# Moving the time operands to the other half of the TensorE array, and reordering the start of a chunked RWKV-7 + MoE kernel

## The chip, the cores and the metric

The kernel runs on one core of a Trainium2 chip, as one launch. The metric is the device time in microseconds; the median of three runs before the change is 947.24 us (946.98 to 950.19).

## The reference

Two blocks run one after the other. The first is an RWKV-7 recurrence over 4 batches, 8 heads, 768 steps and a head size of 40: each head keeps a 40x40 state, which in every step is decayed by `w`, corrected by `a` and `b`, and extended by `v` and `k`; the output of a step reads the state with `r`.

```python
for t in range(S):
    y[:, :, t] = einsum('bhd,bhde->bhe', rt, state)
    Sa = einsum('bhde,bhe->bhd', state, at)
    state = state * wt - outer(Sa, bt) + outer(vt, kt)
```

Its output, 3072 rows of 320, goes through a mixture of 8 experts (320 to 1024, ReLU, and back to 320). The expert of a row is the argmax of its logits, and the result is scaled by the softmax weight of that expert.

## The kernel before, in words

**The recurrence** is computed in 12 chunks of 64 steps. In a chunk the work is split into two units (`s` = 0, 1), each with two batches and eight heads, laid out as 8 groups `g` times two partition halves `par`. A unit's matrices are 64x64 or 64x40 per head. Partition half 0 holds one head and half 1 another, so every small product uses one 64x64 quarter of the 128x128 TensorE array: its rows are given by the partitions of the operands, its columns by the partitions of the output. The helpers `own(par)` and `oth(par)` name a half and the other half. A product that reads `own` and writes `own`, or reads `oth` and writes `oth`, uses one of the two quarters on the array's diagonal; one that reads `own` and writes `oth`, or the reverse, uses one of the two off the diagonal. A step of a unit is a group of 16 products (8 groups, 2 halves); each fp32 product shows in the trace as two MATMULs and two LDWEIGHTS.

**Two streams** are interleaved on TensorE by `weave` (L532), which writes out TensorE's program order by hand. One is the system of the next chunk, `systems` (L571): per unit `ntb`, five steps `level(u, k)`, `couple` and `whole`, 16 groups in all, which invert a triangular 64x64 matrix; the units alternate. `level`, `couple` and `whole` read and write the same half (diagonal quarters); `ntb` is off the diagonal. The other stream is `rest` (L583), 26 groups: `right`, `gtk`, `solve`, `zgram`, `state`, `yield_y`, `atv`, `turned`, `emit`. Two products of `rest` are followed by 16/26 as many of the system.

Before the change `gtk` (L271), `atv` (L289), the first group of `state` (the product of `nk` and `nv`, L450) and the first groups of `yield_y` (with `s_r`, L487, and with `nk` and `AT`, L490) lie on the diagonal, the same quarters as the levels. `right`, `solve`, `zgram` and the second groups of `state` and `yield_y` (with `nb`) lie off it. Where groups from two row halves accumulate into one PSUM bank, `parted` (L212) puts a small ScalarE copy between them, which the second group waits for.

**The chain of a level**: ScalarE copies the new power out of PSUM (L356), VectorE transposes it (`new_n`, L309), VectorE adds the product to the running inverse (L359); the next level of the same unit reads both.

**Decay** (L243) runs ahead for later chunks: a scan on VectorE gives the cumulative decay `PT` (L247), four reciprocals give `wi` (L258), GpSimd multiplies `a` into `ai` (L253) and `k`, `b` into `kb` (L260). `ntb` and `gtk` need `ai` and `kb`.

**The start.** All constants and presets are written on GpSimd: masks, the counters that only the router needs (L87 to L110), zero or one padding of partitions 40 to 63 in the load tiles (L153 to L159), identity columns (L170), zero columns (L173). All input loads are issued on SyncE's queue: per unit 4 for `wp`, 4 for `a`, 8 for `kb` (`load`, L219), 8 for `v` and `ri` (`load_vr`, L231), 40 KB each. Then the system of chunk 0 is woven with `gtk` and `atv` of chunk 0 (L602).

Only TensorE's order is written by hand (`manual_schedule`, L596); on the other engines and queues a planner orders the instructions by when it reckons them ready, earlier code first.

Of the kernel before, what the change touches and what calls it, by code (L numbers as in the profile page):

```python
# [8 lines left out]
F32 = mybir.dt.float32  # L9
# [4 lines left out]
ALU = mybir.AluOpType  # L14
# [3 lines left out]
W, K, A, B_, V, R = range(6)  # L18
# [3 lines left out]
def kernel(  # L22
# [51 lines left out]
    after = consts.tile([128, 128], F32)  # L74
    nc.gpsimd.memset(after[:], 1.0)
    nc.gpsimd.affine_select(
        after[:], after[:], compare_op=ALU.is_gt, fill=0.0, base=0, pattern=[[-1, 128]], channel_multiplier=1,
    )
    ones_sq = consts.tile([128, 128], F32)
    nc.gpsimd.memset(ones_sq[:], 1.0)  # L80
    zero_e = consts.tile([128, E], F32)
    nc.gpsimd.memset(zero_e[:], 0.0)
    keep = consts.tile([128, E, NT], F32)
    nc.gpsimd.memset(keep[:], 1.0)
    nc.gpsimd.memset(keep[:, :, 0:1], 0.0)

    def counted(name, shape, pattern, base, mult=0):  # L87
        ti = consts.tile(shape, I32, name=name + "_i")
        tf = consts.tile(shape, F32, name=name)
        nc.gpsimd.iota(ti[:], pattern=pattern, base=base, channel_multiplier=mult)  # L90
        nc.gpsimd.tensor_copy(tf[:], ti[:])
        return tf

    first_w = counted("first_w", [128, E], [[-1, E]], E)
    b1off = counted("b1off", [128, E], [[CAP, E]], -1)
    b2off = counted("b2off", [128, E], [[-CAP, E]], E * CAP - CAP)
    thr = counted("thr", [128, NX], [[128, NX]], CAP)
    kx = counted("kx", [1, NX], [[1, NX]], 0)
    iota_f = counted("iota_f", [128, 128], [[1, 128]], 0)

    tokv = counted("tokv", [128, NT], [[2 * S, B // 2], [64, S // 64]], 1, 1)
    nc.gpsimd.tensor_scalar(tokv[64:], tokv[64:], scalar1=float(S - 64), scalar2=None, op0=ALU.add)
    iota_r = consts.tile([128, 128], F16)
    nc.gpsimd.tensor_copy(iota_r[:], iota_f[:])

    tok_n = consts.tile([128, NT // 2], F32)
    nc.gpsimd.tensor_scalar(
        tok_n[:], tokv[:, NT // 2 :], scalar1=-1.0, scalar2=float(N // 2), op0=ALU.mult, op1=ALU.add,
    )
    nc.gpsimd.tensor_copy(tokv[:, NT // 2 :], tok_n[:])  # L110
# [8 lines left out]
    with tc.tile_pool(name="ring", bufs=1) as ring, \  # L119
         tc.tile_pool(name="sb", bufs=1) as sb, \  # L120
         tc.tile_pool(name="pp", bufs=1, space=PSUM) as pp:

# [38 lines left out]
        nc.gpsimd.memset(first[:], 0.0)  # L161
        nc.gpsimd.memset(first[:, :, 0:1], 1.0)
# [6 lines left out]
        for t in sum(ai_r + ri_r, []):  # L169
            nc.gpsimd.tensor_copy(t[:, :, T2:], i40[:, None, :].to_broadcast([128, G, D]))  # L170

        for t in sum(nk_r + st_r + s_r + q_r, []):
            nc.gpsimd.memset(t[:, :, D:], 0.0)  # L173
        for t in sum(off_r, []):
            nc.gpsimd.memset(t[:], 0.0)
        for t in sum(x_r, []):
            nc.gpsimd.tensor_copy(t[:], i64[:, None, :].to_broadcast([128, G, T2]))
# [10 lines left out]
        for par in range(2):  # L188
            nc.gpsimd.tensor_copy(iw[own(par), :, :D], i40[own(par), None, :].to_broadcast([64, NP, D]))
# [686 lines left out]
```

## Time and profile before

| | us |
|---|---|
| runs, median of 3 | 947.24 (946.98 to 950.19) |
| profiled execution, its own time | 950.85 |
| span of its instructions | 949.0 |
| PE busy | 847.2 (89%) |
| PEld busy | 659.7 (70%) |
| DVE busy | 404.0 (43%) |
| POOL busy | 281.4 (30%) |
| ACT busy | 261.1 (28%) |

PE is TensorE's matmuls, PEld its weight loads, DVE VectorE, ACT ScalarE, POOL GpSimd, SP SyncE; a q behind a name is the engine's queue issuing. The span runs from the first instruction to the last; the 1.85 us between it and the run's own time lie around it. Matmuls overlap, so a busy PE only says that some matmul was in flight, not how many quarters of the array worked. The page cuts the span into 40 slices of 23.7 us and gives the busy share of each in tenths.

### The profile page before, as it was taken

The numbers are of one execution on the slowest core, as the hardware profiler recorded it, in microseconds if no ns is written. First come the engines' busy times: TensorE is split into PE (matmuls) and PEld (weight loads), VectorE is DVE, ScalarE is ACT, GpSimd is POOL, SyncE is SP. The second block draws the span as 40 slices with busy tenths as digits, with TensorE's granted clock in tenths as the row PEclk, the third lists the DMA queues.
The fourth block names the chain that finished last, engine by engine and source line by source line (L and its number), as shares of the span: only waits on it lengthen the run. The fifth ranks groups of instructions, "written<-read, shape, count | busy, mean of one in ns | idle before, by whom it ended". The sixth has DMA issues, their size and how long they took to land.

```text
span 949.0 us, 37272 instructions
## 1 busy us (share of the span) xinstructions
PE 847.2 (89%) x16828; PEld 659.7 (70%) x16828; DVE 404.0 (43%) x711; ACT 261.1 (28%) x686; POOL 281.4 (30%) x299
## 2 busy tenths in 40 slices
PE   0298798999999999999999991999999999999995
PEld 0288788999999999999999991353635455453633
DVE  1274858584857667585853616210111201011100
ACT  0045252535344353534345330010111001010110
POOL 9634432624325161623422013302113030210101
PEclk9998999999999999999999995799999999999998
DMA  2304132322222232322101008222224131322000
GB/s 63 74 7 91 31 79 51 86 58 59 49 64 63 49 75 46 73 45 59 39 20 38 4 18 245 74 70 92 75 86 146 67 105 63 95 73 62 21 0 22
DMA packets 119605, 60.16 MB, mean 63 GB/s; under 512 B 103825, under 2 KB 115091, under 8 KB 119444
## 3 DMA queue, kind: packets, MB, share of 16 engines
q1 hardware_dynamic: 113236, 48.53, 19.8%
q0 software_dynamic: 3072, 9.20, 3.1%
q8 instruction: 133, 2.18, 1.0%
q10 hardware_dynamic: 3136, 0.01, 0.2%
q14 instruction: 28, 0.23, 0.1%
HBM read 49.83 MB, written 9.19 MB: 62 GB/s over the span
## 4 chain that ended last, share of the span: by engine, by line
PE 38%; issue 35%; POOL 10%; DVE 8%; DMA 3%; ACT 3%; SPq 1%; POOLq 0%; DVEq 0%; ACTq 0%
PE ps_lv L208 12%; PE ps_y L208 6%; POOL out_dram L799 3%; PE ps_ntb L208 3%; PE ps_q L208 3%; POOL xg L761 2%; PE ps_s L208 2%; PE ps_x L208 2%; PE ps_atv L208 2%; PE ps_f L208 2%; PE ps_gtk L208 2%; DVE N L309 2%; DVE pair L359 2%; PE ps_S L208 2%; DVE wi L258 2%
## 5 line engine op out<-in xcount | busy, mean ns | idle before, releaser
L208 PE MATMUL ps_lv<-pair,N 64*64 64x128 f32 (+1 forms) x3840 | 292.8, 256 | 13.2 <-DVE pair L359 8.4
L208 PEld LDWEIGHTS ps_lv<-pair,N 64*64 64x64 f32 x3840 | 249.6, 135 | 18.3 <-issue 12.6
L780 PE MATMUL hp<-xgT,w 128*128 128x512 f32 (+1 forms) x384 | 191.9, 629 | 0.0
L780 PEld LDWEIGHTS hp<-xgT,w 128*128 128x128 f32 (+1 forms) x384 | 63.3, 189 | 123.3 <-issue 122.1
L793 PE MATMUL zp<-w,h_sb 128*128 128x320 f32 x512 | 145.0, 433 | 0.0
L309 DVE STREAM_TRANSPOSE N<-pair 128x512 f32<-128x512 f32 x144 | 101.5, 705 | 96.8 <-ACT pair L356 95.5
L785 DVE TENSOR_SCALAR h_sb<-hp 128x512 f32<-128x512 f32 x32 | 22.1, 692 | 247.1 <-PE hp L780 247.1
L793 PEld LDWEIGHTS zp<-w,h_sb 128*128 128x128 f32 x512 | 94.5, 191 | 34.5 <-issue 0.8
L799 POOL DMA_INDIRECT out_dram<-zo,s_idx x32 | 31.8, 995 | 279.9 <-ACT zo L798 279.9
L208 PE MATMUL ps_ntb<-ai,kb 40*64 40x104 f32 x768 | 73.4, 279 | 45.7 <-POOL kb L260 45.7
L208 PEld LDWEIGHTS ps_ntb<-ai,kb 40*64 40x64 f32 x768 | 61.4, 146 | 46.1 <-POOL kb L260 46.1
L299 POOL TENSOR_TENSOR AT<-AT,up 128x512 f32<-128x512 f32 x24 | 30.5, 1271 | 203.1 <-ACT AT L298 181.1
L258 DVE RECIPROCAL wi<-PT 128x128 f32<-128x128 f32 x96 | 81.6, 907 | 0.6
L356 ACT COPY pair<-ps_lv 128x512 f32<-128x512 f32 x96 | 57.6, 600 | 63.3 <-PE ps_lv L208 52.6
L787 ACT ACTIVATE h_sb<-hp 128x512 f32<-128x512 f32 x32 | 19.1, 597 | 200.5 <-PE hp L780 200.5
L260 POOL TENSOR_TENSOR kb<-kb,wi 128x512 f32<-128x512 f32 x48 | 65.9, 1390 | 26.8 <-DVE wi L258 24.5
L208 PE MATMUL ps_y<-N,off 64*64 64x64 f32 x768 | 63.4, 223 | 5.8 <-DVE N L309 5.7
L208 PE MATMUL ps_gtk<-ai,kb 40*64 40x104 f32 x768 | 68.2, 260 | 0.2 <-issue 0.2
L359 DVE TENSOR_TENSOR pair<-ps_lv,pair 128x512 f32<-128x512 f32 x96 | 63.2, 659 | 8.2 <-PE ps_lv L208 7.3
L208 PEld LDWEIGHTS ps_y<-N,off 64*64 64x64 f32 x768 | 56.2, 133 | 8.2 <-PE ps_y L208 6.2
L208 PE MATMUL ps_atv<-ri,v 40*64 40x104 f32 x768 | 58.5, 251 | 0.2 <-issue 0.2
L208 PEld LDWEIGHTS ps_gtk<-ai,kb 40*64 40x64 f32 x768 | 57.2, 139 | 0.3 <-issue 0.3
(161 smaller groups left out, 1484.8 us busy)
## 6 DMA issues: line engine op xcount, KB each, us to landing
w<-in_moe_w_dram SPq DMA_DIRECT2D x8, 1280.0 KB
w<-in_moe_w_dram SPq DMA_DIRECT2D x8, 1024.0 KB
kb<-in_packed_dram SPq DMA_DIRECT2D x192, 40.0 KB
v<-in_packed_dram SPq DMA_DIRECT2D x96, 40.0 KB
ri<-in_packed_dram SPq DMA_DIRECT2D x96, 40.0 KB
a<-in_packed_dram SPq DMA_DIRECT2D x96, 40.0 KB
wp<-in_packed_dram SPq DMA_DIRECT2D x96, 40.0 KB
x_rows<-xr SPq DMA_DIRECT2D x48, 80.0 KB
```

Of the source, the lines that this page charges most:

```text
L208: nc.tensor.matmul(out_, lhsT=lhs, rhs=rhs, start=start, stop=stop, skip_group_check=free)
L258: nc.vector.reciprocal(wi[:, h, p : p + 2], P4[:, h, p : p + 2, 1:])
L260: nc.gpsimd.tensor_tensor(d["kb"][:, :, i], d["kb"][:, :, i], wi[:], op=ALU.mult)
L299: nc.gpsimd.tensor_tensor(t[:], t[:], up64[:, None, :].to_broadcast([128, G, T2]), op=ALU.mult)
L309: nc.vector.transpose(flat(N[:]), flat(nt))
L356: nc.scalar.copy(new[:, 0], ps[:, :, :T2])
L359: nc.vector.tensor_tensor(new[:, 1], ps[:, :, T2:], pair[:, 1], op=ALU.add)
L780: nc.tensor.matmul(hp[:, :cols], lhsT=g["w"][0][:dsz, db, fb * 128 : (fb + 1) * 128], rhs=g["xT"][:dsz, db, :cols], start=(db == 0), stop= ...
L785: nc.vector.tensor_relu(g["h"][:, fb, :cols], hp[:, :cols])
L787: nc.scalar.activation(g["h"][:, fb, :cols], hp[:, :cols], AF.Relu)
L793: nc.tensor.matmul(zp[:], lhsT=g["h"][:, fb, j * 128 : (j + 1) * 128], rhs=g["w"][1][:, fb, :], start=(fb == 0), stop=(fb == FB - 1),)
L799: ins_ = nc.gpsimd.indirect_dma_start(out=out[:, :], out_offset=bass.IndirectOffsetOnAxis(ap=g["si"](j), axis=0), in_=zo[:], in_offset=Non ...
```

## The change

1. `gtk` and `atv` write to the other half, so their results (`GT`, `nk`, `AT`, `nv`) lie there. By this `gtk`, `atv`, the `nk` groups of `state` and of `yield_y` leave the diagonal; the second group of `right` (with `GT`) comes onto it.
2. The `parted` copies: none in `state` now; two in `right`, between its first and second groups; in `yield_y` between the `s_r` groups and the `nk` groups. The first groups of both units stand ahead in `right` and `yield_y`.
3. Presets: `after` goes; the router's counters are written after the decay of chunk 1 (`routing_constants`); ones of `wp` and the tile `first` are written on VectorE; `a` and the first `kb` buffer are cleared whole on GpSimd; presets not needed by the first products (`off`, `ri`, `xt`, zero columns, the second buffers) come after the decay of chunk 0 (`preset_rest`), those of `iw` after the first weave (`preset_last`).
4. Loads: `wp` first for a unit, then `kb`, then `a`; for chunk 0 `kb` and `a` are issued on ScalarE's queue, `v` and `ri` after the decays.
5. In `decay` the products of `kb` are split by batch, `b` before `k`.
6. In the first weave unit 1 runs one level behind unit 0.

```diff
-            ts = [lambda g=g, par=par: mm(at(own(par), g), kb(d, 0, g)[own(par, D)], d["ai"][own(par, D), g, :])
+            ts = [lambda g=g, par=par: mm(at(oth(par), g), kb(d, 0, g)[own(par, D)], d["ai"][own(par, D), g, :])
...
-            ts = [lambda g=g, par=par: mm(at(own(par), g), d["v"][own(par, D), g, :], d["ri"][own(par, D), g, :])
+            ts = [lambda g=g, par=par: mm(at(oth(par), g), d["v"][own(par, D), g, :], d["ri"][own(par, D), g, :])
...
         def right(us):
-            for u in us:
+            pss = [bank("ps_q", D) for u in us]
+            for u, ps in zip(us, pss):
...
-                        start=(g == 0), stop=False, free=True) for g, par in HD], none
+                        start=(g == 0), stop=False, free=True) for g, par in HD], lambda ps=ps: parted(ps)
+            for u, ps in zip(us, pss):
...
-                    ps[oth(par), g, :], d["GT"][own(par), g, :], d["nv"][own(par), g, :],
+                    ps[oth(par), g, :], d["GT"][oth(par), g, :], d["nv"][oth(par), g, :],
...
         def state(us):
-                    ps[own(par), g, :], d["nk"][own(par), g, :], d["nv"][own(par), g, :],
-                    start=(g == 0), stop=False, free=True) for g, par in HD], lambda ps=ps: parted(ps)
+                    ps[own(par), g, :], d["nk"][oth(par), g, :], d["nv"][oth(par), g, :],
+                    start=(g == 0), stop=False, free=True) for g, par in HD], none
...
         def yield_y(us):
...
-                        start=(g == 0), stop=False, free=True) for g, par in HD], none
-                yield [lambda g=g, par=par: mm(
-                    ps[own(par), g, :], d["nk"][own(par), g, :], d["AT"][own(par), g, :],
-                    start=(c == 0 and g == 0), stop=False, free=True) for g, par in HD], lambda ps=ps: parted(ps)
+                        start=(g == 0), stop=False, free=True) for g, par in HD], lambda ps=ps: parted(ps)
             for u, ps in zip(us, pss):
...
+                yield [lambda g=g, par=par: mm(
+                    ps[own(par), g, :], d["nk"][oth(par), g, :], d["AT"][oth(par), g, :],
+                    start=(c == 0 and g == 0), stop=False, free=True) for g, par in HD], none
...
-        for t in sum(a_r + kb_r, []):
-            for lo in (32, 96):
-                nc.gpsimd.memset(t[lo : lo + 32], 0.0)
-        for t in sum(wp_r, []):
-            for lo in (32, 96):
-                nc.gpsimd.memset(t[lo : lo + 32], 1.0)
-            nc.gpsimd.memset(t[:, :, 0:1], 0.0)
+        for s in range(NB2):
+            nc.vector.memset(wp_r[s][0][:], 1.0)
+            nc.vector.memset(wp_r[s][0][:, :, 0:1], 0.0)
+            nc.gpsimd.memset(a_r[s][0][:], 0.0)
+            nc.gpsimd.memset(kb_r[s][0][:], 0.0)
+            if s == 0:
+                nc.vector.memset(first[:], 0.0)
+                nc.vector.memset(first[:, :, 0:1], 1.0)
...
         def load(u):
             c, s = u
+            q = nc.scalar if c == 0 else nc.sync
...
+                        q.dma_start(d["kb"][own(par, D), b2, i], src[par, :, n])
+                    q.dma_start(d["a"][own(par, D), b2], src[par, :, A])
...
-            for i in range(2):
-                nc.gpsimd.tensor_tensor(d["kb"][:, :, i], d["kb"][:, :, i], wi[:], op=ALU.mult)
+                for i in (1, 0):
+                    nc.gpsimd.tensor_tensor(d["kb"][:, h, i], d["kb"][:, h, i], wi[:, h], op=ALU.mult)
...
             for u in pairs[0]:
                 load(u)
-                load_vr(u)
-                decay(u)
-            weave(systems(pairs[0]), ([lambda u=u, f=f: f(u) for f in (gtk, atv) for u in pairs[0]], 64))
+            for u in pairs[0]:
+                decay(u)
+            for u in pairs[0]:
+                load_vr(u)
+            preset_rest()
+
+            ones, twos = ([lambda u=u: ntb(u)] + [lambda u=u, k=k: level(u, k) for k in range(5)]
+                          + [lambda u=u: couple(u), lambda u=u: whole(u)] for u in pairs[0])
+            order = ones[:2] + [p for pq in zip(twos, ones[2:] + [None] * 2) for p in pq if p]
+            weave((order, 16 * len(order)), ([lambda u=u, f=f: f(u) for f in (gtk, atv) for u in pairs[0]], 64))
+            preset_last()
             for u in pairs[1]:
                 load(u)
                 load_vr(u)
                 decay(u)
+            routing_constants()
```

`routing_constants`, `preset_rest` and `preset_last` hold the instructions that stood at L80 to L110, L170 to L177 and L187 to L192 before, with the second `kb` buffers cleared whole.

## Rows read from the trace of the kernel before

**Rows 1.** The page's slices: PE's busy tenths in 40 slices.

```profile
PE   0298798999999999999999991999999999999995
```

**Rows 2.** Three stretches by windows: length, then each engine's busy time; PEclk; DMA.

```profile
74.56:124.10 49.54, 39.45 (x1221) 38.89 (x1215) 28.56 (x45) 19.65 (x54) 19.77 (x16) 0.93 0.25 56
81.60:88.40 6.80, 6.31 (x155) 6.31 (x158) 1.40 (x2) 2.97 (x9) 2.56 (x3) 0.50 0.46 103
257.20:299.40 42.20, 41.00 (x1352) 40.39 (x1347) 29.05 (x46) 18.54 (x52) 15.68 (x13) 1.00 0.26 59
```

The engines stand in the order PE, PEld, DVE, ACT, POOL; the last two figures are DMA share and GB/s.

**Rows 3.** Groups by line and shape in 257.2 to 299.4, one steady chunk: busy us, mean ns.

```profile
L208 PE MATMUL ps_gtk<-ai,kb 40*64 40x104 f32 x64 | 4.9, 249 | 0.0
L208 PE MATMUL ps_atv<-ri,v 40*64 40x104 f32 x64 | 4.4, 250 | 0.0
L208 PE MATMUL ps_s<-nv,nk 64*64 64x40 f32 x64 | 3.9, 215 | 0.0
L208 PE MATMUL ps_y<-AT,nk 64*64 64x64 f32 x64 | 3.8, 218 | 0.0
L208 PE MATMUL ps_q<-nv,GT 64*64 64x40 f32 x64 | 3.4, 218 | 0.0
L208 PE MATMUL ps_z<-ri,uT 40*64 40x104 f32 x64 | 3.3, 252 | 0.0
L208 PE MATMUL ps_y<-ZT,nb 64*40 64x64 f32 x64 | 2.2, 218 | 0.0
L208 PE MATMUL ps_s<-u,nb 64*40 64x40 f32 x64 | 2.2, 210 | 0.0
```

**Rows 4.** The levels alone beside `state`'s `nk` groups, then its `nb` groups, by windows.

```profile
273.48:277.25 3.77, 3.77 (x40) 2.53 (x36) 0.65 (x1) 0.79 (x2) 1.00 0.31 70
277.25:279.28 2.03, 2.03 (x39) 1.98 (x38) 0.65 (x1) 0.39 (x1) 1.00 0.03 8
```

**Rows 5.** Timeline of ACT and DVE after a level: start, length, instruction, idle before.

```profile
271.17 0.60 ACT L356 COPY pair<-ps_lv 128x512 f32<-128x512 f32 x1
...
271.80 0.71 DVE L309 STREAM_TRANSPOSE N<-pair 128x512 f32<-128x512 f32 x1 [2.98 <-ACT pair L356]
272.44 0.65 DVE L359 TENSOR_TENSOR pair<-ps_lv,pair 128x512 f32<-128x512 f32 x1
```

**Rows 6.** Timeline of POOL over the start.

```profile
4.00 0.52 POOL L155 MEMSET a<- 32x512 f32 x1
...
8.08 7.86 POOL L155 MEMSET kb<- 32x1024 f32 x8
...
20.48 2.17 POOL L170 COPY ai<-i 128x320 f32<-128x320 f32 x4
...
28.71 1.39 POOL L186 TENSOR_SCALAR nup<-before 32x32 f32<-32x32 f32 x4
...
30.94 1.17 POOL L253 TENSOR_TENSOR ai<-a,PT 128x512 f32<-128x512 f32 x1
32.07 2.48 POOL L260 TENSOR_TENSOR kb<-kb,wi 128x512 f32<-128x512 f32 x2
```

**Rows 7.** Timelines of DVE, SP and PE over the start, and ACT's only issues.

```profile
19.90 1.31 DVE L247 TENSOR_TENSOR_SCAN PT<-wp,first 128x520 f32<-128x520 f32 x1 [19.90 <-POOL first L162]
...
38.37 3.38 DVE L258 RECIPROCAL wi<-PT 128x128 f32<-128x128 f32 x4
...
16.52 1.68 SPq L225 DMA_DIRECT2D wp<-in_packed_dram  x4
...
34.61 0.44 PE L208 MATMUL ps_ntb<-ai,kb 40*64 40x104 f32 x2 [34.61 <-POOL kb L260]
44.36 0.44 PE L208 MATMUL ps_ntb<-ai,kb 40*64 40x104 f32 x2 [6.72 <-POOL kb L260]
...
82.09 0.43 PE L208 MATMUL ps_ntb<-ai,kb 40*64 40x104 f32 x1 [4.38 <-POOL kb L260]
...
572.87 2.77 ACTq L648 DMA_DIRECT2D x_rows<-gs  x4
```

More of the change, by code (lines that the diff above doesn't have):

```diff
@@ L87, in counted @@
-    def counted(name, shape, pattern, base, mult=0):
+    numbers = {}
+    def counted(name, shape, *pattern):
         ti = consts.tile(shape, I32, name=name + "_i")
         tf = consts.tile(shape, F32, name=name)
-        nc.gpsimd.iota(ti[:], pattern=pattern, base=base, channel_multiplier=mult)
-        nc.gpsimd.tensor_copy(tf[:], ti[:])
-        return tf
-    first_w = counted("first_w", [128, E], [[-1, E]], E)
-    b1off = counted("b1off", [128, E], [[CAP, E]], -1)
-    b2off = counted("b2off", [128, E], [[-CAP, E]], E * CAP - CAP)
@@ L97 @@
-    thr = counted("thr", [128, NX], [[128, NX]], CAP)
-    kx = counted("kx", [1, NX], [[1, NX]], 0)
-    iota_f = counted("iota_f", [128, 128], [[1, 128]], 0)
+        numbers[name] = ti, tf, pattern
+        return tf
+    first_w = counted("first_w", [128, E], [[-1, E]], E, 0)
+    b1off = counted("b1off", [128, E], [[CAP, E]], -1, 0)
+    b2off = counted("b2off", [128, E], [[-CAP, E]], E * CAP - CAP, 0)
+    thr = counted("thr", [128, NX], [[128, NX]], CAP, 0)
+    kx = counted("kx", [1, NX], [[1, NX]], 0, 0)
@@ L101 @@
+    iota_f = counted("iota_f", [128, 128], [[1, 128]], 0, 0)
     tokv = counted("tokv", [128, NT], [[2 * S, B // 2], [64, S // 64]], 1, 1)
[L102 removed]
     iota_r = consts.tile([128, 128], F16)
[L104 removed]
     tok_n = consts.tile([128, NT // 2], F32)
[L107 to L109 removed]
@@ L110, with routing_constants @@
-    nc.gpsimd.tensor_copy(tokv[:, NT // 2 :], tok_n[:])
+    def routing_constants():
+        nc.gpsimd.memset(ones_sq[:], 1.0)
+        nc.gpsimd.memset(zero_e[:], 0.0)
+        nc.gpsimd.memset(keep[:], 1.0)
+        nc.gpsimd.memset(keep[:, :, 0:1], 0.0)
+        for ti, tf, (pattern, base, mult) in numbers.values():
+            nc.gpsimd.iota(ti[:], pattern=pattern, base=base, channel_multiplier=mult)
+            nc.gpsimd.tensor_copy(tf[:], ti[:])
+        nc.gpsimd.tensor_scalar(tokv[64:], tokv[64:], scalar1=float(S - 64), scalar2=None, op0=ALU.add)
+        nc.gpsimd.tensor_copy(iota_r[:], iota_f[:])
+        nc.gpsimd.tensor_scalar(
+            tok_n[:], tokv[:, NT // 2 :], scalar1=-1.0, scalar2=float(N // 2), op0=ALU.mult, op1=ALU.add,
+        )
+        nc.gpsimd.tensor_copy(tokv[:, NT // 2 :], tok_n[:])
@@ L168 @@
             nc.gpsimd.tensor_copy(i64[own(par)], ident[own(par), own(par)])
[L169 to L177, printed above, removed]
+        for s in range(NB2):
+            nc.gpsimd.tensor_copy(ai_r[s][0][:, :, T2:], i40[:, None, :].to_broadcast([128, G, D]))
         up64 = ring.tile([128, T2], F32, name="up64")
@@ L186, with preset_rest, preset_last @@
                 nc.gpsimd.tensor_scalar(nup[qs, i * 32 : i * 32 + 32], before[qs, qs], scalar1=-1.0, scalar2=None, op0=ALU.mult)
-        iw = ring.tile([128, NP, D + E], F32, name="iw")
-        for par in range(2):
-            nc.gpsimd.tensor_copy(iw[own(par), :, :D], i40[own(par), None, :].to_broadcast([64, NP, D]))
-            nc.sync.dma_start(
-                iw[own(par, D), :, D:], moe_w_gate.rearrange("(p a e) x -> a e p x", p=NP, a=2)[par],
-            )
+        def preset_rest():
+            for s in range(NB2):
+                nc.gpsimd.memset(off_r[s][0][:], 0.0)
+                nc.gpsimd.tensor_copy(ri_r[s][0][:, :, T2:], i40[:, None, :].to_broadcast([128, G, D]))
+                nc.gpsimd.tensor_copy(x_r[s][0][:], i64[:, None, :].to_broadcast([128, G, T2]))
+            for t in [r[0] for r in nk_r + q_r + st_r + s_r] + [r[1] for r in nk_r]:
+                nc.gpsimd.memset(t[:, :, D:], 0.0)
+            for s in range(NB2):
+                nc.gpsimd.memset(kb_r[s][1][:], 0.0)
+                for r in (ai_r, ri_r):
+                    nc.gpsimd.tensor_copy(r[s][1][:, :, T2:], i40[:, None, :].to_broadcast([128, G, D]))
+        iw = ring.tile([128, NP, D + E], F32, name="iw")
+        def preset_last():
+            for par in range(2):
+                nc.gpsimd.tensor_copy(iw[own(par), :, :D], i40[own(par), None, :].to_broadcast([64, NP, D]))
+                nc.sync.dma_start(
+                    iw[own(par, D), :, D:], moe_w_gate.rearrange("(p a e) x -> a e p x", p=NP, a=2)[par],
+                )
         def wide(name):
```

18 lines of the change are left out of this document (4 added, 14 removed).

## The prediction

> **What bounds the kernel now.** I read the page's slices first: PE is busy nine tenths or more from the third slice on, with one dip where the recurrence hands over to the experts, and almost idle in the first slice [rows 1]. So there are three stages: a start without matmuls, the recurrence, the experts. The change touches the first two.
>
> In the recurrence, windows by chunk show 42.2 us for a steady one, 41.0 of them with a matmul in flight, while VectorE has 29.05 us of work, ScalarE 18.54 and GpSimd 15.68, at a granted clock of 1.00 [rows 2]. A busy PE does not say how full the array is, so the next view groups the same chunk by product and shape; each row there stands for two groups of 16 products, one per unit. Products of one shape differ by where they lie. `gtk` and `zgram` are both 40x104; on the levels' quarters `gtk` takes 4.9 us, off them `zgram` takes 3.3. The two products of `state` take 3.9 us on the levels' quarters (with `nk`) and 2.2 off them (with `nb`); those of `yield_y` 3.8 and 2.2 [rows 3]. Is it the levels that give way instead? No: beside `nk` they ran 40 instructions in 3.77 us, beside `nb` 39 in 2.03 [rows 4]. In one quarter two streams add up; in different quarters they overlap. That is the loop's limit: diagonal quarters hold the levels and five products of `rest`, the other two stand half empty.
>
> At the start TensorE waits until 34.61 us for GpSimd's `kb`, then for unit 1's until 44.36 [rows 7]. GpSimd's presets stand in front of that product [rows 6].
>
> **A steady chunk.** Each product that leaves the diagonal is priced by its twin of the same kind off it [rows 3]: `gtk` 4.9 - 3.3 = 1.6 us; `atv` 4.4 - 3.3 = 1.1; `nk` of `state` 3.9 - 2.2 = 1.7; `nk` of `yield_y` 3.8 - 2.2 = 1.6. The sum is 6.0. The second group of `right` goes onto the diagonal, but it stands beside `ntb`, which is off it, so it gains too: at most 3.4 - 2.2 = 1.2 by the nearest product of 40 columns; part of it now meets a level, and I take 0.3 (bounds -0.5 and 1.2). Together 6.3 us.
>
> What is late next is the chain of a level. ScalarE's copy starts at 271.17, the addition ends at 272.44 + 0.65 = 273.09 [rows 5]: 1.92 us, and with about 0.4 for the end of the matmul and the hand-overs some 2.3 (an estimate from these rows). Meanwhile TensorE has one level of the other unit, 32 instructions, which beside a product in other quarters take 2.03 x 32/39 = 1.67 us [rows 4]. Where `rest` stretches that to more than 2.3 nothing waits: a 40x104 group at 3.3/2 = 1.65 us, with 26/16 of them per level, makes 2.7. Beside groups of 2.2/2 = 1.1 us it makes 1.8, below 2.3. Once per two levels 2.3 - 1.67, about 0.65, is then lost. By order, levels 2 and 4 come to stand beside such groups; they give back 2 x 0.65 = 1.3 us. Net 6.3 - 1.3 = 5.0 per chunk, so 37.2 us, which leaves VectorE's 29.05 as cover. Ten weaves have this form (chunks 1 to 10 with the next chunk's system): 50 us. In the last chunk no system runs, so nothing is freed: 0.
>
> The number of `parted` copies stays at four a chunk; in `right` and `yield_y` the other unit's group of 1.1 us or more stands between a group and its `parted` partner, which covers it. Without that cover each costs the wait for its 16 products, 1.1 us, four times. ScalarE, which issues them in order, has 42.2 - 18.54 = 23.7 us free [rows 2].
>
> **The skill, weighed.** The rows above show levels and `nb` products overlapping although each pair shares the array's row half. The Trainium skill, page "TensorE: Matmul & The Clock Gate", section "Part 3: Packing small matmuls", says that a weight load overlaps matmuls in flight only when their row group differs. By that rule the move would free nothing, for it changes the column half alone, and the loop's sum would be 0 instead of 50. The rows of `state` disagree with it here; it stays a rival below.
>
> **The first two weaves.** The system of chunk 0 is bound by its chain (30.2 us from 44.36 to 74.56 for at most 20 groups), with only 4 groups of `rest` to move: 0. Unit 1 one level behind lets `level 0` of unit 0 run before `ntb` of unit 1; I take 0, bounds -2 and +2. The next weave took 49.54 us, with PE busy 39.45 [rows 2]: a wait of 4.38 us for unit 1's `kb` [rows 7] and 6.8 us at clock 0.50 [rows 2], which at half speed is worth 3.4. Decays of chunk 1 come as late after the first weave's chain as before, so I let both stand and take half a steady chunk's gain, 2.5 (bounds 0, and 5.0 + 4.4 + 3.4 = 12.8).
>
> **The start.** GpSimd goes on doing the two masks (ready before 2 us), four clears in front: two `a` at 0.52, two `kb` at 7.86/8 = 0.98, 3.0 us; two identity copies at 2.17/4 = 0.54; the small masks, 1.39 and some 1.5 for what goes with them [rows 6]. That is 9 us in place of 30.94. The other six `kb` strips (5.9), the `wp` and `first` padding, the router's counters and the later presets leave the front. VectorE's padding is not in the trace; the nearest row is GpSimd's clear of a like number of columns, 0.52, so 2 us for all, at a time when VectorE waits until 19.90 anyway [rows 6, 7].
>
> So the loads decide. The first `kb` may be issued once it is cleared, near 3.2 us. On ScalarE's queue an issue costs between 1.68/4 = 0.42 us, as on SP, and 2.77/4 = 0.69, its only rows, which are of another transfer [rows 7]. The SP rows have the same 40 KB, so I lean to them: 12 issues are done at 8.2, unit 1's 12 at 13.3 (at 0.69: 11.5 and 19.8). Landing takes some 2 us (an estimate: `wp` issued at 16.52 to 18.2 was scanned at 19.90). Then `ai` 1.17 and three half products of `kb`, 3 x 0.62: unit 0's `ntb` near 13.3, unit 1's data at 15.3. Unit 1's reciprocals, 3.38 us, stood behind unit 0's first result on VectorE before [rows 7]; if they do again, from 16.5 on, `kb` is ready near 21. Unit 1's `ntb` at 21 instead of 44.36 makes 23.4 us. The bounds: 28 where the reciprocals go first, 12 with issues at 0.69 and the later presets on GpSimd (some 20 clears and copies of 0.2 to 1 us, by the like rows of before) ahead of the sum that the second level needs.
>
> **Edits costed at nothing.** The order `wp`, `kb`, `a` on SP in the loop: same count, and the loads are a chunk ahead. Splitting `kb`: eight half products for four whole ones cost some 0.1 us each on an engine that is idle 26 us a chunk. The router's counters are a few us of GpSimd work that the router needs only after the recurrence; in front of chunk 2's products they would delay those by as much, on an engine with 26 us to spare.
>
> **Sum.** 50 + 2.5 + 23.4 = 76 us (75.9). The profiled execution took 950.85 us (span 949.0), so it would be 875; the median is 3.6 lower, and the same saving gives 871.3.
>
> **The rivals.**
> - *The levels' chain takes it back* (0.17). Were a foreign copy of 0.60 us [rows 5] ahead of each level's copy on ScalarE, the chain takes 2.9. Levels 2 and 4 lose 1.25 each, levels 1 and 3 0.25, `couple` and `whole` 0.6 each: 4.0. Then 2.3 us a chunk is left, 23 in ten, with 2.5 and 23.4: 898. For it: a shorter chunk packs ScalarE denser. Against: 18.54 of 37.2 us is half.
> - *The start gives less* (0.11): 12 instead of 23.4, 883.
> - *More than forecast* (0.11): nothing given back (63), the start 28, and the second weave's waits gone (12.8): 104 less, 843.
> - *The move does nothing* (0.03), by shared rows of the array as above: 23.4 alone, 924.
> - *Slower, by the clock* (0.03). At 0.50 the clock stood right after the 4.38 us wait of TensorE at 77.7 to 82.1 [rows 2, 7]. If the waits that the faster streams open let it fall in the loop, each us there costs half a us; from 2 x 76 = 152 us at the lower level on the gain is gone, and with all ten chunks (372 us) there it comes to 871 + 186 = 1057. Against it: steady chunks wait already and stood at 1.00, and the waits I expect are of 0.65 us.
>
> The forecast itself has 0.55. Range 845 to 905: it takes in the first two rivals and all but the end of the third. What a measurement here can tell from no change is 0.5%, 4.7 us; only the last rival is slower (0.03), and I leave 0.02 for no change, so 0.95 for faster.
>
> **What would show it.** In a steady chunk: about 37 us; `gtk`, `atv` near 3.3, the two `nk` products near 2.2; more waits of `ps_lv` on VectorE. `ntb`'s first matmuls near 13 and 21 us. A chunk of 40 us or more with the twins at 3.3 and 2.2 means the chain took it; twins unchanged mean that shared rows bind; a clock below 1.00 in the loop means the last rival. The experts' stretch stays as long as it was.

## The result, and the profile after

The changed kernel took 924.67 us, median of four runs (917.44 to 945.18), against 948.72 for the kernel before beside it: a ratio of 0.9717 [0.9641, 0.9793]. A later comparison on another chip gave 933.83 (eight runs, 920.85 to 951.44) against 951.2, 0.9821 [0.9797, 0.9846]. Ratios are formed from the runs within 1.5% of the fastest of their kernel, medians from all, so the two can differ. Faster, but not by 76 us, and outside the forecast range of 845 to 905. The runs lie further apart than those of the kernel before (947 to 954), and their order is nearly that of TensorE's mean granted clock: 920.85 us at 0.971, 933.25 at 0.956, 951.44 at 0.928. That is part of the answer.

The profiled execution took 917.44 us (span 915.7). The page's slices of it, PE's busy tenths and the granted clock, and its line on the queue that brings instructions:

```profile
PE   0677879888999898888989945999999999999995
PEclk9999999999977999999999975999999999999998
...
q8 instruction: 133, 2.18, 1.0%
```

PE fills six tenths of the second slice where it filled two [rows 1], but in the recurrence it shows 8s where it had 9s: it stands still more. Two slices of the loop have a lower clock.

Windows by chunk, with the columns of [rows 2]: the second weave, an undisturbed chunk, two that met the lower clock, and another undisturbed one.

```profile
64.60:106.50 41.90, 33.50 (x1231) 32.06 (x1229) 30.69 (x47) 18.64 (x50) 18.75 (x20) 0.96 0.29 65
...
189.90:230.20 40.30, 36.21 (x1353) 34.33 (x1348) 28.14 (x44) 18.39 (x51) 14.88 (x15) 1.00 0.28 62
230.20:275.20 45.00, 41.28 (x1354) 39.42 (x1353) 29.09 (x47) 19.07 (x53) 19.18 (x21) 0.87 0.25 55
275.20:319.20 44.00, 39.68 (x1351) 38.33 (x1349) 28.54 (x45) 18.31 (x51) 14.01 (x13) 0.90 0.25 56
...
442.10:481.80 39.70, 36.06 (x1355) 34.33 (x1354) 19.89 (x37) 18.98 (x53) 12.80 (x13) 1.00 0.13 29
```

Before, the ten chunks behind the second weave took 41.6 to 46.8 us, six of them in a row 42.2 to 42.8, always at 1.00. After, those at 1.00 take 39.1 to 41.9, and two take 45.0 and 44.0. By stage the profiled execution gained: 10.0 us up to the second weave (74.6 before, 64.6 after), 7.7 in that weave (49.6 to 41.9), 14.4 in the ten chunks behind it (428.8 to 414.4) where 50 had been forecast, 0.9 in the last; the experts' stretch is as long as it was.

Did the products that were moved get faster? The groups of [rows 3] in the chunk 442.1 to 481.8:

```profile
L215 PE MATMUL ps_z<-ri,uT 40*64 40x104 f32 x64 | 3.3, 251 | 0.2 <-issue 0.2
L215 PE MATMUL ps_gtk<-ai,kb 40*64 40x104 f32 x64 | 3.2, 251 | 0.0
L215 PE MATMUL ps_atv<-ri,v 40*64 40x104 f32 x64 | 3.2, 251 | 0.0
L215 PE MATMUL ps_q<-nv,GT 64*64 64x40 f32 x64 | 2.7, 224 | 0.0
L215 PE MATMUL ps_y<-ZT,nb 64*40 64x64 f32 x64 | 2.5, 218 | 0.1
L215 PE MATMUL ps_y<-AT,nk 64*64 64x64 f32 x64 | 2.4, 223 | 0.0
L215 PE MATMUL ps_s<-nv,nk 64*64 64x40 f32 x64 | 2.3, 227 | 0.0
L215 PE MATMUL ps_s<-u,nb 64*40 64x40 f32 x64 | 2.1, 211 | 0.0
```

They did, close to their prices: `gtk` 3.2, `atv` 3.2, the `nk` products 2.3 and 2.4, `q` 2.7 where 3.1 was reckoned. So the time is lost between the products. The waits of the weight loads in a chunk (us in total, times, longest), first before, 257.2 to 299.4:

```profile
PEld ps_y L208 <- PE ps_y L208: 0.8, 1, 0.8
PEld ps_lv L208 <- ACT u L438: 0.3, 1, 0.3
PEld ps_lv L208 <- issue: 0.3, 1, 0.3
PEld ps_y L208 <- PE ps_lv L208: 0.3, 1, 0.3
```

and after, 189.9 to 230.2:

```profile
PEld ps_lv L215 <- issue: 3.1, 5, 1.3
PEld ps_y L215 <- issue: 2.1, 3, 1.5
PEld ps_lv L215 <- ACT nb L342: 0.5, 1, 0.5
PEld ps_gtk L215 <- issue: 0.3, 1, 0.3
```

1.7 us of waits became 6.0, while the chunk went from 42.2 to 40.3: without waits 40.5 became 34.3, which is 6.2 freed of the forecast 6.3. But 5.5 us are now put down to "issue", a wait for nothing that the profile shows on an engine. One of them (1.5 us, at 221.91) is a wait for VectorE's `N` in PE's own list; most of the others are something new. One of the new kind, from the timeline (start, length, instruction, idle before), with its weight load:

```profile
460.10 0.49 PE L215 MATMUL ps_lv<-pair,N 64*64 64x128 f32 x5
461.45 0.32 PE L215 MATMUL ps_lv<-pair,N 64*64 64x128 f32 x2 [0.86 <-issue]
...
461.45 0.13 PEld L215 LDWEIGHTS ps_lv<-pair,N 64*64 64x64 f32 x2 [1.11 <-issue]
```

and the only transfer on any queue from 459.10 to 460.30 (packets, MB, share of the 16 engines):

```profile
q8 instruction: 1, 0.02, 4.6%
```

PE stops inside a group of products whose operands are all there, while a packet of instructions has just come: it ended at 460.03 by the trace's records, 1.42 us before PE went on. On the page q8 moved 133 packets and 2.18 MB, 16.4 KB each; PE and its weight loads have 2 x 16828 = 33,656 instructions, 253 for each packet, and 256 with those of PE's sequencer (34,001 records). Counted through all these records, the six stops of this kind in the chunk 189.9 to 230.2 (they end at 197.08, 201.10, 208.63, 211.97, 216.18 and 219.62; 3.0 us together) lie 255 to 257 or 512 instructions apart, and each ends 1.36 to 1.51 us after the end of a q8 packet, and these packets take 0.9 to 1.5 us. The same count finds none in the chunk 257.2 to 299.4 before. So TensorE waits for its own instructions: in this chunk the next packet begins 0.7 to 1.8 us after the first instruction of a block of 256, and when the block runs out before the packet has come and some 1.4 us more have passed, PE stops. Before, 256 instructions ran for 40.5/2706 x 256 = 3.8 us; now they take 34.3/2701 x 256 = 3.25 us, and in the recurrence no two packets end less than 3.3 us apart.

How much is that in the whole loop? The profile of the later comparison (the execution of 920.85 us) tells it best, since in its ten chunks the clock stood at 0.50 for 3.4 us only. The ten chunks in one window, before and in that execution of the change:

```profile
124.10:552.80 428.70, 413.21 (x13451) 405.48 (x13447) 277.58 (x438) 185.97 (x519) 148.12 (x114) 1.00 0.24 53
...
109.50:524.00 414.50, 363.55 (x13449) 345.06 (x13445) 273.01 (x433) 187.09 (x520) 151.16 (x147) 1.00 0.24 53
```

The weight loads were busy for 405.5 us and are for 345.1: 60.4 us were freed, of 63 forecast. They stand idle for 23.2 us before and 69.4 after. Of this the refill stops (idle times of 0.1 us or more at that place in the count by 256) have 3.2 us before, in 10 stops, and 42.3 after, in 65; everything else has 20.0 and 27.1. So 39.1 us went to the refill and 7.1 to other waits, and 14.2 were left. The first profile, with 58 stops of 32.6 us and 20.5 us at the lower clock, comes to the same 14.4.

### The profile page after: what moved, and what is told of

Same layout as the page of the kernel before. It is cut to its first block, busy times and chain, and to the rows that moved or that the text cites. A ratio compares the mean times of both kernels' runs of the same rounds, so it can differ in the third digit from the quotient of the medians.

```text
span 915.7 us, 37348 instructions
## 1 busy us (share of the span) xinstructions
PE 795.1 (87%) x16828; PEld 596.1 (65%) x16828; DVE 406.3 (44%) x717; ACT 261.0 (29%) x684; POOL 280.9 (31%) x331
## 3 DMA queue, kind: packets, MB, share of 16 engines
q8 instruction: 133, 2.18, 1.0%
## 4 chain that ended last, share of the span: by engine, by line
issue 37%; PE 36%; DVE 9%; POOL 9%; DMA 4%; ACT 3%; SPq 1%; POOLq 0%; DVEq 0%; ACTq 0%
PE ps_lv L215 12%; PE ps_y L215 5%; POOL out_dram L820 3%; PE ps_ntb L215 3%; DVE pair L369 3%; PE ps_q L215 3%; PE ps_f L215 2%; PE ps_x L215 2%; POOL xg L782 2%; DVE N L319 2%; PE ps_S L215 2%; PE ps_gtk L215 2%; DVE PT L257 2%; PE ps_atv L215 1%; PE ps_z L215 1%
## 5 line engine op out<-in xcount | busy, mean ns | idle before, releaser
L215 PE MATMUL ps_lv<-pair,N 64*64 64x128 f32 (+1 forms) x3840 | 251.8, 261 | 38.5 <-DVE pair L369 19.0
L215 PEld LDWEIGHTS ps_lv<-pair,N 64*64 64x64 f32 x3840 | 227.2, 135 | 48.7 <-issue 33.3
L270 POOL TENSOR_TENSOR kb<-kb,wi 128x256 f32<-128x256 f32 x96 | 75.9, 811 | 180.3 <-DVE wi L268 110.3
L215 PE MATMUL ps_ntb<-ai,kb 40*64 40x104 f32 x768 | 65.0, 279 | 27.6 <-POOL ai L263 27.6
L215 PE MATMUL ps_y<-N,off 64*64 64x64 f32 x768 | 51.2, 238 | 12.4 <-DVE N L319 9.6
L215 PE MATMUL ps_f<-pair,xt 64*64 64x64 f32 x768 | 56.5, 238 | 0.9 <-ACT xt L386 0.8
L215 PEld LDWEIGHTS ps_y<-N,off 64*64 64x64 f32 x768 | 46.2, 135 | 15.8 <-issue 11.0
L819 ACT ACTIVATE zo<-zp,xg 128x320 f32<-128x320 f32 x32 | 16.9, 527 | 132.0 <-PE zp L814 128.2
L215 PE MATMUL ps_gtk<-ai,kb 40*64 40x104 f32 x768 | 52.3, 259 | 0.9 <-issue 0.9
L215 PEld LDWEIGHTS ps_f<-pair,xt 64*64 64x64 f32 x768 | 48.0, 140 | 1.5 <-ACT xt L386 1.2
```

What stands on the lines that cost most here:

```text
L215: nc.tensor.matmul(out_, lhsT=lhs, rhs=rhs, start=start, stop=stop, skip_group_check=free)
L270: nc.gpsimd.tensor_tensor(d["kb"][:, h, i], d["kb"][:, h, i], wi[:, h], op=ALU.mult)
```

## The experiments

**Theories.** F: these refill stops give back what the streams free. K: waits, bunched, bring the granted clock down in the loop. Rivals: C, the levels' chain gives it back, as the prediction had it; W, a wait costs only what it lasts; S and L for the start (below). Ratios are to the kernel before on the same chip.

**The two parts alone.** `halves_only` is the kernel before with the array-half edits; `start_only` is the change with the old halves.

```
 start_only:  -  mm(at(oth(par), g), kb(d, 0, g)[own(par, D)], ...
              +  mm(at(own(par), g), kb(d, 0, g)[own(par, D)], ...   # and so in atv, right, state, yield_y
```

> The kernel before with the array-half moves alone (gtk, atv, right, state, yield_y as in the changed kernel; presets, loads and the first weave as before). It divides the gain. In the two traces the stretch from the first weave's end to the experts is 494.8 us before and 471.8 after: this kernel should show some 472 there and start as before, so about 23 us less than before: 920 to 930. Theory F (TensorE's instructions come in blocks of 256, about one per 3.55 us, and the faster stream now waits for them) and theory C (the chain of a level takes the gain back) both expect this; F expects the new waits at every 256th instruction, C at the first matmul of a level. If the clock falls in the loop as it did at 264 us after the change, up to 15 us more.

> The changed kernel with the old array halves (gtk, atv, right, state, yield_y as before). The first weave ended 10.0 us earlier after the change (64.6 for 74.6), and the second lost no 4.4 us wait: 8 to 18 us less than before, 930 to 940, with steady chunks of 42.2 us as before. Both theories expect that.

`start_only` 933.8 (0.9829 [0.9797, 0.9862]), chunks of 42.2 at 1.00 as before: the start is worth 16.7 us. `halves_only` 962.6, 1.0108 [1.0062, 1.0154]: **slower** than before, where 920 to 930 had been expected, up to 945 with the clock. Four of its windows:

```profile
228.00:271.40 43.40, 40.48 (x1355) 39.50 (x1351) 27.98 (x45) 18.60 (x51) 13.07 (x10) 0.87 0.25 57
271.40:311.70 40.30, 36.21 (x1349) 34.28 (x1346) 29.05 (x47) 18.76 (x53) 15.90 (x14) 1.00 0.28 62
311.70:357.50 45.80, 41.70 (x1355) 39.98 (x1353) 28.73 (x45) 19.20 (x53) 17.95 (x14) 0.87 0.24 54
401.50:443.90 42.40, 36.47 (x1355) 34.44 (x1353) 28.67 (x45) 19.29 (x53) 16.48 (x13) 1.00 0.26 59
```

Behind the second weave a chunk at 1.00 takes 39.5 to 42.4; a fall to 0.50 inside makes 43.0 to 52.0. In all 116 us of its recurrence ran at 0.50, against 7 before.

**Instructions.** `after_twice` issues each product of `gtk`, `atv`, `zgram` and `solve` again, one column wide (512 more instructions a chunk); `merged` joins the products of `state` and `yield_y` that share a stationary operand (256 fewer).

```
 after_twice: +  mm(out[..., :1], lhs, rhs[..., :1])     # behind each product of the four
 merged:      -  ps_s <- nk, nv   and   ps_y <- nk, AT   (nb, u and nb, ZT likewise)
              +  ps_sy <- nk, [AT | nv]                  # 104 columns
```

> The changed kernel, each product of gtk, atv, zgram and solve issued a second time for its first column only (the same value again). 128 more products a chunk are 512 more instructions and almost no array time, all of it on the quarters off the diagonal, which have room. F: two more blocks of 256 a chunk at 3.55 us, 7.1 us in each of 11 to 12 chunks: 55 to 85 us more than the changed kernel, 980 to 1010, with waits at every 256th instruction. C: at most 5 us a chunk of short passes on quarters that are half empty, mostly hidden: 0 to 15 us more, 925 to 940.

> The changed kernel with state and yield_y made one: nk times [AT, nv] and nb times [ZT, u] as products of 104 columns in place of 64 and 40 apart. The same columns pass through the array, 64 products and so 256 instructions a chunk fall away; VectorE has two more short instructions a unit. F: one block less per chunk, 3.55 us where every block is waited for: 20 to 38 us less than the changed kernel, 887 to 905. C: the chain of the levels is untouched and VectorE has more to do: 0 to 10 us more, 925 to 935.

`after_twice` 1030.27, over both forecasts (102 us of its recurrence ran at 0.50, against 24 in the change). A chunk at 1.00, and one that met the low clock:

```profile
215.60:263.10 47.50, 44.15 (x1613) 42.68 (x1611) 29.51 (x45) 19.11 (x53) 16.24 (x17) 1.00 0.23 53
...
365.50:427.00 61.50, 60.36 (x1610) 59.71 (x1608) 29.32 (x44) 19.05 (x51) 14.48 (x14) 0.68 0.18 41
```

Its five chunks at 1.00 take 46.8 to 48.3 us, the change's eight 39.1 to 41.9: by their means 7.0 us for 512 instructions, some 14 ns each, near the rate of all the others (34.3 us for 2701 makes 12.7). So an instruction costs its place in the order, however little it computes, and C, which expected 0 to 15 us in all, is out as the main cause; but the stops themselves hardly grew (at 1.00 on the mean 3.7 us a chunk against 3.3, by the count above), so this run shows the price of an instruction rather than that of a refill. `merged` 949.31, 0.994 [0.9902, 0.9979]: both forecasts missed, since most of its chunks had the clock at 0.74 to 0.91. At 1.00, its last full chunk took 37.80 us against 39.10 in the change: the direction of F, but a single chunk.

**The start.** Both forms put GpSimd into program order, with the routing counters behind the second chunk and part of the padding on VectorE; `old_start_pool` has the old halves.

```
 -  with tc.manual_schedule(engines={PE}):
 +  with tc.manual_schedule(engines={PE, Pool}):
```

> The changed kernel with GpSimd kept in program order: the first unit's kb and ai products directly behind the presets it needs, the routing constants behind the second chunk, the remaining copies and the padding of the second kb buffer on VectorE. Theory S (the start is late because GpSimd, busy without a break from 0.8 to 27 us, has presets and constants between the products): first ntb product about 16 us (24.1 in the changed kernel), the second unit's about 24 (34.9), the loop's start 7 to 10 us earlier, 908 to 918 us. Rival L (the loads of kb and a set the start, and GpSimd only fills the time): first ntb not before 21, 920 to 926.

> The same start with all array-half edits undone, so the loop is that of the kernel before. Theory S: 7 to 10 us under the run with the changed start alone (933.8), so 923 to 927 us; rival L: 930 to 935. Theory K (the granted clock) expects 1.00 through the whole loop here, and little spread between the runs.

Why the start came late, by the change's own timeline of GpSimd, where [rows 6] had the clears:

```profile
18.49 0.44 POOL L190 COPY ai<-i 128x320 f32<-128x320 f32 x1
18.90 0.72 POOL L270 TENSOR_TENSOR kb<-kb,wi 128x256 f32<-128x256 f32 x1
19.57 0.44 POOL L190 COPY ri<-i 128x320 f32<-128x320 f32 x1
19.96 0.69 POOL L196 COPY iw<-i 64x160 f32<-64x160 f32 x2
20.72 0.72 POOL L270 TENSOR_TENSOR kb<-kb,wi 128x256 f32<-128x256 f32 x1
21.39 0.20 POOL L97 MEMSET ones_sq<- 128x128 f32 x1
...
22.84 1.16 POOL L263 TENSOR_TENSOR ai<-a,PT 128x512 f32<-128x512 f32 x1
```

and PE's first products of the two units, which answer to [rows 7]:

```profile
24.06 0.96 PE L215 MATMUL ps_ntb<-ai,kb 40*64 40x104 f32 x8 [24.06 <-POOL ai L263]
...
34.92 0.79 PE L215 MATMUL ps_ntb<-ai,kb 40*64 40x104 f32 x6 [3.54 <-POOL ai L263]
```

The planner laid later presets, the gate's copy and the routing counters between the products, and `ai`, which every `ntb` needs, behind them. With GpSimd in order (`start_pool`) the first `ntb` came at 16.1 us and unit 1's at 23.9, where 16 and 24 had been expected: S was right about the cause. Yet the times were 940.73 (0.9826 [0.9722, 0.993]) and 933.76 (0.9836 [0.9785, 0.9887]), no better than without. In the second weave of `old_start_pool` TensorE waits:

```profile
PE ps_lv L217 <- POOL pair L346: 7.3, 1, 7.3
PE ps_ntb L217 <- POOL kb L272: 4.3, 1, 4.3
```

In program order the sum `pair` that a level needs stands behind the `ai` and `kb` products of the chunk after next. The weave, which began 9.1 us earlier than in `start_only` (56.5 against 65.6), took 62.3 us in place of 45.0. Besides these waits 30 us of it ran at 0.50 (3.4 in `start_only`); what each of the two cost was not told apart.

**Waits in the y stage.** The long falls of the clock in the ten chunks (13 us and more) began in the last third of a chunk in all profiles, but for one in `after_twice`; in the change's at 263.7. The next runs took it that PE waits there for ScalarE's `seen` copy. `filled` puts a group of `atv` behind that copy; `sr_first` moves the first y groups ahead of `state`, `old_first` does the like under the old halves, with the `AT` groups moved too.

```
 filled:    yield_y, first groups;  + atv(next unit 0);  yield_y, other groups
 sr_first:  + ps_y <- ri, s (both units);  state;  yield_y without them
```

> The changed kernel with one piece of independent work moved: the first atv group of the next chunk stands between the first and the second y groups, where PE waits 0.3 to 1.9 us for ScalarE's seen copy before each fall of the clock. Theory K (the granted clock falls to 0.50 because waits bunch in the y stage; each fall costs 4 to 8 us): the clock stays at 1.00 through the loop, chunks of 39.5 to 40.5 us, 898 to 912 us. Theory F alone (instruction refill sets the pace, and filled waits return as refill stops): 915 to 922, refill stops longer, clock as in the changed kernel. Rival: the atv group finds its PSUM buffers held, no gain: 922 to 930.

> The changed kernel with the first y groups (state times r) moved ahead of the state groups, so that ScalarE's seen copies run beside four groups of state and PE no longer waits 0.3 to 1.9 us for them in the y stage. Theory K (waits that bunch in the y stage bring the granted clock to 0.50, at 4 to 8 us a fall): no or one fall in the loop, chunks of 39.5 to 40.5 us, 900 to 912 us. Theory F alone (refill of instructions sets the pace; a wait removed comes back as a refill stop): 915 to 922, falls as in the changed kernel. Rival: the wait moves to the buffers that state now takes later, 922 to 930.

> The kernel with the changed start alone and the old array halves (933.8 us), with the same reordering: the y groups that end in a seen copy ahead of the state groups. Its y stage waits 0.37 and 0.9 us a chunk: without them 41.0 a chunk and 920 to 926 us, clock 1.00 in the loop. If the halves are worth anything once the clock holds, the reordered changed kernel is 8 to 25 us under this one; by F at its strongest (floor 3.5 us for 256 instructions, some 37.4 us a chunk) at least 5.

`filled` 927.72, 0.9759 [0.9691, 0.9827], mean clocks 0.926 to 0.959, no better than the change. Its premise does not hold: the change's profile puts no wait of TensorE down to `seen`; behind the copies at 253.2 and 255.2, in the weave of the fall, TensorE does not stand still for 0.15 us or more until 256.8, and 1.9 us is the longest of ScalarE's own idle times before such a copy. Just ahead of the fall stand a refill stop (0.6 us in PE's list, ended at 261.12) and a wait of `couple` for VectorE's `N` (0.7 us, ended at 263.30); such a wait of 1.5 us at 221.91 was followed by no fall. So this run says nothing for or against waits. `sr_first` 925.5, 0.971 [0.9657, 0.9762]: no gain that can be told from the change. `old_first` 955.45, 1.0043 [1.0023, 1.0062], a miss of 30 us in the forecast: a level now waits up to 1.1 us for VectorE's `pair`, and its chunks take 44.1. With the first y groups ahead of `state`, then, the new halves are worth 30 us; in the old order (933.8 against 924 to 934) less than 10.

Is it a wait at all? `long_wait` and `long_wait2` made the copy behind the AT groups longer; the other unit's products covered it, TensorE's steady chunks stayed at 41.8 to 42.9, and the times (937.95 and 938.16), under every forecast, tell nothing. `gated` put the wait into TensorE's order:

```
 +  nc.scalar.activation(gate, junk, Copy, scale=0.0)      # behind two copies of the last AT tile
 +  mm(ps_y, gate, AT)                                     # adds 0, once a chunk
```

> The kernel with the changed start alone (933.8 us, clock 1.00 in the loop) with the one-element seen copy behind each AT group of y replaced by two copies of the whole 128x512 tile on ScalarE, 1.2 us for each of two waits in a chunk; TensorE's program is the same. Theory W (a wait costs what it lasts): 2 to 2.4 us a chunk, 953 to 962 us, clock 1.00. Theory K: with 3 to 4 us of waits close together in the y stage the granted clock falls to 0.50 in most chunks, 47 to 50 us a chunk, 975 to 1010 us.

> The kernel with the changed start alone (old halves, 933.8 us, clock 1.00 in the loop) with one more product a chunk between the AT and the ZT groups of y: its stationary operand is 64x64 zeros that ScalarE writes behind two copies of the last AT group's 128x512 tile, so PE stands still for about 0.15 + 2 x 0.6 + 0.4 us and the semaphores, some 2 us, once a chunk (0.37 us was waited there before). Theory W (a wait costs what it lasts): 1.5 to 2 us a chunk, 950 to 960 us, clock 1.00 in the loop. Theory K (a pause of this length together with the waits around it brings the clock to 0.50): falls in most chunks, 46 to 50 us a chunk, 975 to 1010 us.

956.2, 1.0071 [1.0048, 1.0093], with chunks of 43.2 to 45.9 at 1.00, on the mean 2.0 us over those of `start_only`: that is W, and K as I had put it falls under the old halves. Under the new ones no run made a wait longer. The product behind the wait, in the timeline of `gated`:

```profile
276.73 0.27 PE L215 MATMUL ps_y<-AT,gate 64*64 64x64 f32 x1 [1.72 <-ACT gate L226]
```

Around that wait, by windows; the clock held:

```profile
271.00:277.80 6.80, 5.08 (x184) 4.94 (x181) 2.71 (x5) 2.31 (x6) 0.00 (x0) 1.00 0.15 34
```

A stretch of the same length in `halves_only`, just before a fall at 478.6:

```profile
471.80:478.60 6.80, 5.16 (x220) 4.86 (x221) 6.77 (x10) 2.42 (x8) 1.27 (x1) 1.00 0.12 27
```

PE was as busy in the one as in the other (5.08 and 5.16 us), and issued more products where the clock fell. How long it stands still does not tell these two stretches apart.

**Columns.** `wider40` gives the change 64 moving columns in place of 40 in 148 products of a chunk; `halves_wider` does it to `halves_only`, `sr_wider` to `sr_first`.

```
 -  mm(ps[..., g, :], nk, nv[..., g, :])                 # 40 columns
 +  mm(ps[..., g, :64], nk, flat(nv)[g*40 : g*40 + 64])  # also q, nb.u, turned; the extra 24 are unused
```

> The changed kernel with 64 moving columns in place of 40 in 160 products of a chunk (both q groups, both state groups, the turned state); the extra columns are not used, instructions, waits and buffers stay. 24 columns are some 41 ns of stream (109 ns for 64 by the levels), 6.5 us a chunk end to end, 3.3 with two array halves side by side. Theory F (PE has spare stream time between refills of 256 instructions): most of it is absorbed, refill stops get shorter, chunks at clock 1.00 stay 39.7 to 41.5, 915 to 932 us. Rival theory stream (PE's streams set the pace and the stops only show where it is ahead): 3 us a chunk, 950 to 965 us.

> The array-half edits alone on the kernel before (962.6 us, mean clock 0.92 to 0.943) with 64 moving columns in place of 40 in the q, state and turned-state products. If wider operands hold the clock: mean clock 0.95 or more and 940 to 952 us, although TensorE has more to stream. If they don't matter: 957 to 968 us at the same clock.

> The changed kernel with both the first y groups ahead of state and 64 columns in place of 40. If each helps the clock on its own account: 0.97 and 913 to 921 us, under both the kernel before and the change (924.7). If the runs of the two differed only by chance: 921 to 930 us.

`wider40` 924.4, 0.9726 [0.9686, 0.9767]: the columns cost nothing. Its chunks at 1.00:

```profile
197.20:237.40 40.20, 35.93 (x1356) 34.22 (x1352) 28.16 (x44) 18.41 (x51) 14.75 (x14) 1.00 0.28 62
237.40:278.80 41.40, 36.20 (x1356) 34.27 (x1348) 28.72 (x47) 18.65 (x52) 16.67 (x18) 1.00 0.27 60
```

Not for the reason that I had given: the stops did not get shorter (2.7 to 7.0 us a chunk); products beside each other took no longer with 64 columns than with 40, which fits a pace set by their instructions. And `halves_wider`, which has more to compute than `halves_only` and the same order, took 943.58 in place of 962.6, 0.9932 [0.9897, 0.9967] against 1.0108 [1.0062, 1.0154], at a mean clock of 0.960 to 0.968 in place of 0.92 to 0.943 (on another chip; the kernel before took 949.72 there and 950.5 beside `halves_only`):

```profile
213.60:254.80 41.20, 36.34 (x1353) 34.30 (x1349) 27.95 (x44) 18.42 (x51) 14.68 (x12) 1.00 0.27 60
254.80:296.90 42.10, 36.63 (x1357) 34.62 (x1354) 29.07 (x47) 19.08 (x53) 16.35 (x14) 1.00 0.27 59
...
380.10:422.90 42.80, 37.67 (x1356) 35.74 (x1349) 28.50 (x45) 18.97 (x52) 16.40 (x14) 0.96 0.26 58
```

The 19 us go with the clock: the recurrence ran 31 us at 0.50 in place of 116, and the refill stops are still there (39.7 us in the ten chunks). The y stage of `halves_wider`, in a chunk where the clock held, against the row of `halves_only` above:

```profile
323.50:330.30 6.80, 4.47 (x191) 4.02 (x183) 6.76 (x11) 1.86 (x6) 1.04 (x1) 1.00 0.17 37
```

PE was even less busy there (4.47 us), with wider products.

**A version that beats both.** `sr_wider` took 920.02, 0.9684 [0.9635, 0.9734]. Beside the change on one chip:

> The changed kernel, timed beside the next one on one chip. If the clock is what spreads its runs: mean clocks from 0.92 to 0.97, times from 917 to 945 us that follow them, median 922 to 930 us.

> The changed kernel with the first y groups ahead of state and 64 columns in place of 40. If wider operands hold the clock: all runs at 0.96 to 0.98 and 914 to 924 us, median 3 to 8 us under the changed kernel's on the same chip. If not: the same spread and a median within 2 us.

The change 933.83, 0.9821 [0.9797, 0.9846]; `sr_wider` 920.5 (917.14 to 927.58), 0.9702 [0.9667, 0.9738], clocks of 0.963 to 0.975 against 0.928 to 0.971. The intervals don't meet: unused columns and the new order of the y stage together make the changed kernel 13 us faster, and its runs more alike. Which of the two does it is not shown; on another chip each alone took 924.4 and 925.5.

## Why the prediction was wrong, step by step

- *Where the limit lay.* Right: twins off the diagonal priced the moved products, and they came out close to those prices. In the ten chunks 60.4 us were freed, 63 forecast. The rule of shared rows that was weighed ("TensorE: Matmul & The Clock Gate", "Part 3: Packing small matmuls", in the Trainium skill) is at odds with the rows after as well: `gtk` and `atv`, whose row half stayed, went from 4.9 and 4.4 us to 3.2. The `nk` groups are no test of it: they changed their row half and not the column half, which the prediction overlooked when it took the rows of `state` against the rule.
- *What is late next.* This is the step that failed: "What is late next is the chain of a level", with 1.3 us a chunk given back, and no term for the supply of TensorE's instructions. All waits other than refill stops grew by 7.1 us in the ten chunks, where the chain had been given 13; the refill stops grew by 39.1, where the sum had nothing. The source was on the page: 133 instruction packets for 33,656 instructions, a block of which lasted only 3.8 us. The Trainium skill, page "Runtime: NRT & Kernel Launch", section "Instruction fetch mechanics", says that an engine's instructions are refilled in blocks of 16 KiB, 256 instructions, and that crossing a boundary is "mostly hidden". The size agrees (16.4 KB, 253 a packet); nearly hidden it was before the change (3.2 us in ten chunks), and is no longer at 12.7 ns an instruction. The prediction's own sign, "A chunk of 40 us or more with the twins at 3.3 and 2.2 means the chain took it", came true and would have misled.
- *The clock.* The last rival had the effect at 0.03, from the rows at 81.60 to 88.40 [rows 2], and dismissed it because steady chunks wait already. In the profiled execution 20.5 us of two chunks ran at 0.50; they took 44.0 and 45.0, together some 7 to 8 us over their neighbours. In the second comparison an execution at 0.952 took 13.6 us longer than that at 0.971 (934.41 and 920.85). That waits are its cause is not shown: a pause of 1.7 us did nothing under the old halves. Nor is the clock what kept the loop from its forecast, since the ten chunks that met it for 3.4 us gained no more (14.2 us) than those that met it for 20.5 (14.4).
- *The start.* 23.4 forecast up to the second weave; 10.0 came in the profile, 8.8 in that of `start_only`, whose 16.7 us have the second weave in them too. The loads were later than forecast: the issues on ScalarE's queue ended at 18.5 us (13.3 forecast, 19.8 the bound), and with GpSimd in order the first `ntb` waited for `kb` to land until 16.1 (13.3 forecast). What set the start of the changed kernel was "presets leave the front": the planner put them between the products again, since no one waits for them by name. Unit 1's `ntb` came at 34.92, not 21.
- *The second weave.* 2.5 forecast, 7.7 in the profile, and 4.7 in `start_only` without the new halves: half of the lower clock (6.8 to 3.4 us) and part of the 4.38 us wait went.
- *Edits costed at nothing.* Not right for the routing counters, which went into the start. The halves of the split `kb` product take 0.72 us where 0.62 had been half of a whole one, the 0.1 us that was said. The order of the loads was not run alone.
- *Sum.* 16.7 for the start and 6.1 for the halves where the clock mostly holds (`halves_wider`, 949.72 to 943.58) make 22.8; the change gave 24.0 in the first comparison and 17.4 in the second. That the measured 924.67 is the number of the rival "The move does nothing" (924) is chance, for the move did what it was priced at. In the rival of the chain the items add up to 4.2 us, not 4.0.

Open: which quantity the clock follows. With wider products it held better in `halves_wider` than in `halves_only`, and a wait alone did not bring it down under the old halves; more is not shown. Nor did a run change the refill by itself: that PE waits for it rests on the place of the stops in the count by 256 and on their end behind a packet.

## What to carry to other kernels

Before streams are made to overlap, divide the time that they leave by the number of TensorE's instructions: here about 12.7 ns an instruction, and 3.3 us between two packets of 256, were about the least that was reached, and 40 columns cost as much as 64. Behind a change that makes TensorE's work lighter, read the granted clock of each stretch and of several executions first; a theory of waits is cheap to form, and here it began with one that TensorE did not have. An edit that moves work out of a planner's way has to be looked up in the order that results.

## What the hardware showed beyond that

- The same array-half edits were 1.1% slower or 0.7% faster than the kernel before, without or with 24 unused columns in 148 products of a chunk (on two chips).
- A one-column product costs TensorE about as much of its order as a full one: some 14 ns for each of its instructions.
- TensorE's stops for its next instructions went from 3.2 us in ten chunks to 32.6 and 42.3 when the same number of instructions ran in less time.
- A stop of 1.7 us for ScalarE's `gate`, in every chunk, left the granted clock at 1.00 in the loop; under the new halves it fell behind a stretch in which PE was as busy.
